# Attention followed by a gated feed-forward layer on one core: all transposes of rows and attention outputs move to TensorE

## The chip, the core and the metric

The kernel runs on one core of one Trainium2 chip. A core has five engines that run side by side, each with its own queue of instructions that it takes in order: TensorE (PE, matrix products and transposes, results in PSUM), VectorE (DVE), ScalarE (ACT), GpSimd (POOL), and SyncE (SP), which here only issues DMA transfers. The metric is the device time of one execution in microseconds (us), lower is better. The profile was taken from one execution by the hardware profiler.

## What is computed

The reference, cut to what matters (batch 8, 12 heads, 448 positions, head size 64; model size 768, inner size 2048):

```python
q_n, k_n = rmsnorm(q, g_q), rmsnorm(k, g_k)          # x / sqrt(mean(x*x) + 1e-6) * g
scores = q_n @ k_n.T / sqrt(64)
attn = softmax(scores)
x = (attn @ v)                                       # to (8*448, 768)
h = x @ w_in                                         # 768 -> 2048
out = (h * sigmoid(1.702 * h)) @ w_out               # 2048 -> 768, float32
```

Inputs are float32; the products are made in bfloat16 with float32 sums.

## The kernel before, in words

**Pairs.** The 8 x 12 heads are worked on as 48 pairs, `i` = 0 to 47, six pairs to a batch. The 128 partitions hold two heads of 64 where the head size lies on the partitions. A position is split as `ss * 4 + ns`, with 112 `ss` on the partitions and four `ns` along the row, so that 448 positions fill 112 partitions.

**One pair.** `load` (L869 for q and k, L867 for v) brings q, k and v, 224 KB each. `square` (L873 on POOL, L878 on ACT) and `reduce` (L887, DVE) give the sums of squares, and `seed`/`rsqrt` (or `by_log` for the first six pairs) one over the root. `norm` (L931, POOL or DVE) scales the rows and writes them as bfloat16 into a ring of three row buffers, `row_ring`. Rows have positions on the partitions; the score product needs the head size there. So each row buffer is **turned**: `T` in the plan, eight blocks of 112 x 128, four of Q and four of K.

- Pairs 0 to 11 (`ON_PE = NP * 2`): `turn_pe` (L954) does it by PE transposes into a PSUM bank, then two DVE copies bring it to SBUF: `take_q` (L958, called `KQ`) and `take_k` (L961, called `K`), the latter with the gains `gG` as a scale.
- Pairs 12 to 47: `turn_dma` (L966) issues one transposing DMA on SP, from the row buffer straight to SBUF. `scale_q` then multiplies Q by the gains in SBUF, on ACT (L973) or DVE (L975); this is `KQ` for these pairs.

`score` (`C`, L1001) multiplies Q and K on PE, `expo` (`E`, L1009 or L1011, ACT) takes the exponential, `values` (`P`, L1022, PE) multiplies by V with a column of ones that gives the sum, and `divide` (`O`, L1032 and L1033, DVE) writes the quotient into one of two buffers `obs`. The feed-forward layer needs this output turned once more (`B` and `X`): pairs 0 to 11 by `back_pe` (L1048, PE transposes into PSUM) and `take_x` (L1052, a DVE copy), pairs 12 to 47 by `back_dma` (L1055), one transposing DMA on SP.

**Feed-forward.** `first` (`F`, L1229) makes the 2048 inner columns of a batch in 16 groups, `tanh` (`H`, L1240, ACT) and `gate` (`G`, L1252, DVE) the gate. Tokens of two batches at a time go through `w_out`, plainly (`second`, L1260) or by a seven-product scheme on 2 x 2 blocks (`product`, L1325, with sums on DVE, L1316). The last two batches make `F` by such a scheme too (L1614). Results are copied out of PSUM by ACT or DVE and stored by SP (L1283).

**PSUM.** Two double banks hold scores, one bank `o` holds value products, and three banks `w` (two at the start) serve everything else: `F`, the output products, PE turns. A user holds its bank until its last reader is done: a PE turn of rows from the first transpose to the end of `K`, a turn back to the end of `X`. After the attention the score banks join the `w` banks.

**The order.** Nothing is scheduled on the fly. `ORDER` lists, engine by engine, every task's name in the order of its issue; `od.add` gives each task a cost, its dependencies and the PSUM or buffer slot that it takes, and `_Order.run` walks the lists with these costs. What comes out is the order in which the instructions are emitted, which free bank a task gets, and the filler matmuls (`fill`, L845) that go where the walk sees PE idle in the first 45 us. A name that stands in another engine's list than its `add` gives (`alt`) is made by that engine. The chip's times come from the chip: the lists fix only the order on each engine, and semaphores do the waiting.

Of the kernel before, what the change touches and what calls it, by code (L numbers as in the profile page):

```python
# [11 lines left out]
ALU = mybir.AluOpType  # L12
# [16 lines left out]
APART = 45000.0  # L29
APART = 45000.0  # L30
APART = 70000.0


class _Order:
# [36 lines left out]
    def run(self):  # L71
# [15 lines left out]
        lanes = []  # L87
# [37 lines left out]
        def begin(t):  # L125
# [4 lines left out]
            if t.eng == "POOL":  # L130
                when = max(when, hold)
            elif t.moves and len(lanes) >= LANES:
                when = max(when, lanes[-LANES].end)
# [12 lines left out]
        while emitted < len(self.tasks):  # L146
# [40 lines left out]
            if t.moves:  # L187
                t.rest, t.end = t.moves, NEVER
                t.there = free[eng] + (LANDS_SW if eng == "POOL" else LANDS)
                queues[{"POOL": "sw", "ACT": "act"}.get(eng, "hw")].append(t)  # L190
                if eng != "POOL":
                    lanes.append(t)
            else:
                finish(t, free[eng] + t.lat)
# [9 lines left out]
    def open(self, name, now):  # L204
# [5 lines left out]
        ('R', 0, 0), ('R', 0, 1), ('R', 1, 0), ('R', 1, 1), 'g', ('KQ', 0), 'gG', ('R', 3, 0),  # L210
        ('K', 0), ('R', 2, 0), ('N', 3, 0), ('N', 3, 1), ('KQ', 1), ('K', 1), ('V', 0), ('R', 4,
        0), ('KQ', 2), ('K', 2), ('V', 1), ('KQ', 3), ('K', 3), ('O', 0, 0, 0), ('R', 5, 0),
        ('X', 0, 0), ('O', 1, 0, 0), ('KQ', 4), ('K', 4), ('V', 3), ('O', 2, 0, 0), ('V', 4),
        ('X', 1, 0), ('KQ', 5), ('O', 3, 0, 0), ('X', 2, 0), ('V', 5), ('K', 5), ('O', 4, 0, 0),
        ('X', 3, 0), ('X', 4, 0), ('O', 0, 1, 0), ('R', 6, 0), ('R', 7, 0), ('X', 0, 1), ('O',
        5, 0, 0), ('X', 5, 0), ('R', 8, 0), ('Q0', 8), ('O', 1, 1, 0), ('G', 0, 0), ('X', 1, 1),
        ('G', 0, 2), ('O', 2, 1, 0), ('N', 6, 0), ('G', 0, 3), ('G', 0, 1), ('O', 3, 1, 0),
        ('X', 2, 1), ('KQ', 6), ('K', 6), ('G', 0, 4), ('O', 4, 1, 0), ('G', 0, 5), ('X', 3, 1),
        ('KQ', 7), ('K', 7), ('X', 4, 1), ('O', 5, 1, 0), ('V', 6), ('X', 5, 1), ('G', 0, 6),
        ('R', 9, 0), ('G', 0, 7), ('G', 0, 8), ('KQ', 8), ('K', 8), ('R', 10, 0), ('R', 11, 0),  # L220
        ('Q0', 11), ('G', 0, 10), ('O', 6, None, 0), ('G', 0, 9), ('V', 7), ('O', 7, None, 0),
        ('G', 0, 12), ('G', 0, 11), ('O', 7, None, 1), ('G', 0, 13), ('V', 8), ('G', 0, 14),
        ('KQ', 9), ('K', 9), ('R', 12, 0), ('G', 0, 15), ('O', 6, None, 1), ('KQ', 10), ('R',
        13, 0), ('K', 10), ('X', 6, None), ('R', 14, 0), ('O', 8, None, 0), ('Q0', 14), ('O', 9,
        None, 1), ('KQ', 11), ('K', 11), ('O', 8, None, 1), ('X', 7, None), ('R', 15, 0), ('X',
        8, None), ('R', 16, 0), ('O', 9, None, 0), ('V', 10), ('R', 17, 0), ('V', 11), ('Q0',
        17), ('O', 11, None, 0), ('X', 9, None), ('O', 11, None, 1), ('KQ', 13), ('O', 10, None,
        0), ('O', 10, None, 1), ('R', 18, 0), ('O', 12, None, 1), ('X', 10, None), ('R', 19, 0),
        ('X', 11, None), ('R', 20, 0), ('Q0', 20), ('N', 17, 0), ('O', 12, None, 0), ('G', 1,
        1), ('G', 1, 0), ('V', 14), ('N', 18, 1), ('G', 1, 2), ('G', 1, 3), ('O', 13, None, 1),  # L230
        ('TT', 0, 1), ('G', 1, 4), ('TT', 0, 0), ('TT', 1, 0), ('G', 1, 5), ('TT', 2, 0), ('G',
        1, 7), ('O', 13, None, 0), ('G', 1, 6), ('R', 21, 0), ('G', 1, 8), ('O', 14, None, 0),
        ('G', 1, 9), ('TT', 1, 1), ('TT', 3, 0), ('O', 14, None, 1), ('G', 1, 11), ('G', 1, 10),
        ('O', 15, None, 1), ('TT', 2, 1), ('G', 1, 12), ('TT', 3, 1), ('G', 1, 13), ('O', 15,
        None, 0), ('G', 1, 14), ('G', 1, 15), ('R', 22, 0), ('KQ', 18), ('S1', 0, 3), ('O', 16,
        None, 0), ('R', 23, 0), ('Q0', 23), ('S2', 0, 3), ('S3', 0, 3), ('U', 0, 3, 0), ('O',
        16, None, 1), ('X2', 0, 3), ('S4', 0, 3), ('O', 17, None, 1), ('N', 21, 0), ('X3', 0,
        3), ('S1', 0, 5), ('U', 0, 4, 1), ('O', 17, None, 0), ('X1', 0, 5), ('R', 25, 0), ('R',
        24, 0), ('U', 0, 3, 1), ('O', 18, None, 1), ('S2', 0, 5), ('R', 26, 0), ('KQ', 21),
        ('S3', 0, 5), ('Q0', 26), ('U', 0, 5, 0), ('O', 18, None, 0), ('S4', 0, 5), ('U', 0, 6,  # L240
        1), ('O', 19, None, 0), ('G', 2, 0), ('U', 0, 5, 1), ('R', 28, 0), ('O', 19, None, 1),
        ('R', 27, 0), ('G', 2, 2), ('V', 21), ('O', 20, None, 1), ('G', 2, 1), ('R', 29, 0),
        ('G', 2, 4), ('N', 26, 0), ('Q0', 29), ('G', 2, 3), ('O', 20, None, 0), ('G', 2, 5),
        ('G', 2, 6), ('G', 2, 7), ('O', 21, None, 0), ('R', 30, 0), ('G', 2, 8), ('V', 22),
        ('G', 2, 9), ('G', 2, 10), ('O', 21, None, 1), ('R', 31, 0), ('G', 2, 11), ('O', 22,
        None, 0), ('G', 2, 12), ('O', 22, None, 1), ('G', 2, 13), ('KQ', 26), ('N', 29, 0),
        ('G', 2, 14), ('G', 2, 15), ('O', 23, None, 1), ('R', 32, 0), ('S1', 1, 0), ('Q0', 32),
        ('S2', 1, 0), ('O', 23, None, 0), ('U', 1, 0, 0), ('S3', 1, 0), ('V', 25), ('O', 24,
        None, 1), ('R', 33, 0), ('O', 24, None, 0), ('X3', 1, 0), ('U', 1, 1, 1), ('O', 25,
        None, 0), ('U', 1, 2, 0), ('S4', 1, 0), ('KQ', 28), ('U', 1, 1, 0), ('N', 31, 1), ('V',  # L250
        26), ('O', 25, None, 1), ('G', 3, 0), ('R', 34, 0), ('U', 1, 0, 1), ('G', 3, 2), ('O',
        26, None, 1), ('R', 35, 0), ('G', 3, 1), ('G', 3, 3), ('G', 3, 4), ('O', 26, None, 0),
        ('Q0', 35), ('G', 3, 6), ('G', 3, 5), ('G', 3, 7), ('O', 27, None, 1), ('G', 3, 9),
        ('R', 37, 0), ('O', 27, None, 0), ('G', 3, 10), ('G', 3, 8), ('O', 28, None, 1), ('R',
        36, 0), ('G', 3, 12), ('G', 3, 11), ('O', 28, None, 0), ('R', 38, 0), ('Q0', 38), ('G',
        3, 13), ('O', 29, None, 0), ('G', 3, 14), ('G', 3, 15), ('S1', 1, 3), ('S2', 1, 3),
        ('U', 1, 3, 0), ('O', 29, None, 1), ('KQ', 32), ('S3', 1, 3), ('O', 30, None, 1), ('S4',
        1, 3), ('S5', 1, 2), ('X3', 1, 3), ('O', 30, None, 0), ('S1', 1, 5), ('U', 1, 4, 1),
        ('U', 1, 2, 1), ('KQ', 33), ('U', 1, 3, 1), ('S2', 1, 5), ('O', 31, None, 0), ('X1', 1,
# [402 lines left out]
def kernel(  # L662
# [22 lines left out]
    HALF = DM // 2  # L685
    WIN = 128
    AW = (NS - 1) * SS + WIN
    ON_PE = NP * 2
    EARLY = 4
    FILL, FILL_GAPS = 1.2, 0.6  # L690
    SINGLE = NP
# [1117 lines left out]
```

## Time and profile before

| what | value |
|---|---|
| median of 3 runs | 410.34 us (409.89 to 411.89) |
| the profiled execution | 410.82 us |
| its span, first to last instruction | 409.0 us |
| PE busy | 399.9 us, 98% |
| DVE, ACT, POOL busy | 308.1 (75%), 295.6 (72%), 197.7 us (48%) |
| PE transposes of rows, of outputs | 96 and 48 |
| transposing DMAs | 36 of rows, 36 of outputs |
| filler matmuls | 81, 11.8 us |
| granted PE clock | 0.999 |

A page of the profile gives the busy time of each engine, the span in 40 slices, the chain of work that ended last, and the costliest groups of instructions, each named by engine, line, operation and tiles. Other views give an engine's waits (who was waited for, total, number of times, longest), busy time by stretch of the span, and the timeline. PE's matmuls overlap each other: the duration of one is from its start to its modelled end, and the pace is read from start to start.

### The profile page before, as it was taken

What the parts mean: (1) busy time and instruction counts of PE and PEld (TensorE: products, weight loads), DVE (VectorE), ACT (ScalarE), POOL (GpSimd) and SP (SyncE); (2) the same over time, 40 slices, a digit from 0 to 9 for tenths busy, and PEclk for the clock granted to TensorE, in tenths of its full rate; (3) what the DMA queues carried; (4) which work ended last, traced back from release to release, by engine and by line L of the source; (5) the groups of instructions that cost most, each with busy time, mean ns of one, the idle gap of its engine ahead of it and who ended that gap; (6) DMA issues with size and microseconds to landing.
All of it is one profiled execution on the core that took longest, in us unless ns stands there. A gap on an engine that the chain in (4) does not pass through costs nothing.

```text
span 409.0 us, 9973 instructions
## 1 busy us (share of the span) xinstructions
PE 399.9 (98%) x3842; PEld 236.1 (58%) x3842; DVE 308.1 (75%) x624; ACT 295.6 (72%) x445; POOL 197.7 (48%) x289
## 2 busy tenths in 40 slices
PE   7899999999999999999999999999999999999996
PEld 6567886565555555555555555455455665555664
DVE  3997887778998597967686789887776788755353
ACT  4998899799898879766885668778888534685121
POOL 6787878874449657465884469343511200000000
PEclk9999999999999999999999999999999999999999
DMA  8999999999468977757766678656543113000244
GB/s 221 265 238 212 265 230 242 186 204 232 111 167 196 207 178 195 193 141 192 171 148 156 170 155 195 155 146 149 127 121 89 46 43 96 2 1 2 77 131 141
DMA packets 101776, 63.38 MB, mean 155 GB/s; under 512 B 55008, under 2 KB 101728, under 8 KB 101728
## 3 DMA queue, kind: packets, MB, share of 16 engines
q1 hardware_dynamic: 91840, 53.98, 54.7%
q0 software_dynamic: 7360, 6.29, 9.6%
q10 hardware_dynamic: 2528, 2.47, 2.3%
q8 instruction: 30, 0.49, 0.5%
q14 instruction: 18, 0.15, 0.2%
HBM read 45.61 MB, written 11.01 MB: 138 GB/s over the span
## 4 chain that ended last, share of the span: by engine, by line
PE 88%; DMA 6%; DVE 3%; ACT 1%; POOL 1%; SPq 0%; issue 0%; ACTq 0%; DVEq 0%; POOLq 0%
PE w L1229 25%; PE w L1325 22%; PE o L1022 12%; PE sc L1001 10%; PE b L1325 7%; PE b L1614 5%; PE w L1260 4%; DMA rows<-in_q_dram 3%; PE w L1614 3%; DMA rows<-in_k_dram 3%; DVE ssq L887 1%; PE w L954 1%; PE w L1048 1%; DVE g L1252 1%; ACT sq L878 0%; DVE obs L1033 0%
## 5 line engine op out<-in xcount | busy, mean ns | idle before, releaser
L1009 ACT ACTIVATE att<-sc 112x896 bf16<-112x896 f32 x168 | 145.8, 918 | 31.3 <-PE sc L1001 29.9
L1229 PE MATMUL w<-xt,w_in_s 128*128 128x448 bf16 (+1 forms) x672 | 121.5, 326 | 0.0
L1022 PEld LDWEIGHTS <-att 112*128 112x128 bf16 x1536 | 66.1, 98 | 34.2 <-issue 13.3
L1229 PEld LDWEIGHTS <-w_in_s 128*128 128x128 bf16 x672 | 60.2, 97 | 38.2 <-issue 5.0
L931 POOL TENSOR_TENSOR row<-rows,rs 112x512 bf16<-112x512 f32 x70 | 74.9, 1089 | 13.8 <-DMA qk<-row 9.7
L1252 DVE SCALAR_TENSOR_TENSOR g<-th,w 128x448 bf16<-128x448 f32 x96 | 58.0, 616 | 14.9 <-ACT th L1240 14.5
L1240 ACT ACTIVATE th<-w 128x448 f32<-128x448 f32 x96 | 50.9, 550 | 20.0 <-PE w L1229 16.5
L1022 PE MATMUL o<-vx,att 112*128 112x65 bf16 x1280 | 64.5, 194 | 0.6 <-DVE obs L1033 0.5
L887 DVE TENSOR_REDUCE ssq<-sq 112x16 f32<-112x1024 f32 (+1 forms) x50 | 57.9, 1168 | 6.6 <-ACT sq L878 5.7
L873 POOL TENSOR_TENSOR sq<-rows 112x512 f32<-112x512 f32 x37 | 39.7, 1090 | 21.4 <-DMA rows<-in_q_dram 12.5
L1001 PE MATMUL sc<-qk 64*128 64x448 bf16 (+1 forms) x360 | 47.4, 342 | 1.4 <-DVE qk L961 1.2
L944 POOL TENSOR_TENSOR vx<-rows,ones 112x512 bf16<-112x512 f32 x21 | 22.3, 1065 | 48.7 <-PE o L1022 40.8
L1033 DVE TENSOR_TENSOR obs<-o,rcp 112x256 bf16<-112x256 f32 x96 | 40.8, 425 | 3.3
L1325 PEld LDWEIGHTS <-late 128*128 128x128 bf16 x312 | 28.3, 97 | 19.7 <-issue 2.9
L1325 PEld LDWEIGHTS <-g 128*128 128x128 bf16 x288 | 26.0, 97 | 19.1 <-issue 4.0
L1032 DVE RECIPROCAL rcp<-o 112x4 f32<-112x4 f32 x96 | 17.2, 179 | 25.9 <-PE o L1022 25.2
L878 ACT ACTIVATE sq<-rows 112x1024 f32<-112x1024 f32 (+1 forms) x27 | 27.2, 1012 | 5.5 <-DMA rows<-in_q_dram 5.4
L1325 PE MATMUL w<-w_out_s,g 128*128 128x384 bf16 x152 | 29.4, 326 | 0.0
L920 POOL TENSOR_TENSOR t<-rs 112x48 f32<-112x48 f32 x28 | 9.2, 328 | 34.3 <-DVE rs L908 29.2
L1325 PE MATMUL w<-late 128*128 128x384 bf16 x136 | 25.7, 326 | 0.0
L1325 PE MATMUL w<-w_out_s,late 128*128 128x384 bf16 x128 | 24.1, 326 | 0.0
L1011 ACT ACTIVATE att<-sc 112x896 bf16<-112x896 f32 x24 | 20.6, 916 | 0.9 <-PE sc L1001 0.7
(133 smaller groups left out, 509.6 us busy)
## 6 DMA issues: line engine op xcount, KB each, us to landing
rows<-in_v_dram SPq DMA_DIRECT2D x42, 224.0 KB, 3.8
rows<-in_k_dram SPq DMA_DIRECT2D x41, 224.0 KB, 3.6
rows<-in_q_dram SPq DMA_DIRECT2D x41, 224.0 KB, 4.0
w_in_s<-in_moe_w_in_dram POOLq DMA_DIRECT2D x4, 768.0 KB, 10.7
w_out_s<-in_moe_w_out_dram POOLq DMA_DIRECT2D x4, 768.0 KB, 14.6
out_dram<-osb SPq DMA_DIRECT2D x14, 144.0 KB, 3.1
out_dram<-osb SPq DMA_DIRECT2D x10, 168.0 KB, 3.1
out_dram<-osb SPq DMA_DIRECT2D x11, 120.0 KB, 2.3
```

What stands on the lines that cost most here:

```text
L873: made = [nc.gpsimd.tensor_tensor(out=sq[i % N_SQ][:SS, g], in0=raw[turn(i, N_RAW, K_RAW)][:SS, g], in1=raw[turn(i, N_RAW, K_RAW)][:SS, g] ...
L887: nc.vector.reduce_sum(out=ssq_of[g0][:SS, i - g0, part], in_=sq[i % N_SQ][:SS, part], axis=AX.X)
L931: return eng.tensor_tensor(out=row_ring[i % N_QKN][:SS, gi].rearrange("p n (h d) -> p h n d", h=2), in0=raw[turn(i, N_RAW, K_RAW)][:SS, gi ...
L1001: nc.tensor.matmul(sc[:, hp, j * SH:j * SH + n], lhsT=qkw[r, k0:k0 + WIN], rhs=qk[r, 0, qs], start=True, stop=True)
L1009: nc.scalar.activation(out=att[:SS, t, :, :S], in_=sc, func=ACT.Exp)
L1022: nc.tensor.matmul(os_[u, w][:, x, :], lhsT=att_of(u)[:SS, kc, hp, qs * SS:qs * SS + WIN], rhs=vx_ring[turn(i, N_V, K_V)][:SS, hp, kc, :], ...
L1033: nc.vector.tensor_tensor(out=to[:SS, :, w, :] if h is None else to[:SS, :2].rearrange("p n h d -> p (n h) d"), in0=o[:SS, :, :D], in1=rcp ...
L1229: nc.tensor.matmul(gps[b, m][:, j * SH:j * SH + n], lhsT=w_in_s[:, ki, f * 128:(f + 1) * 128], rhs=xT[b][:, ki, lo:lo + n], start=(ki == 0 ...
L1240: nc.scalar.activation(out=th[:, :], in_=gps[b, m][:, :S], func=ACT.Tanh, scale=0.851)
L1252: nc.vector.scalar_tensor_tensor(out=g_of[b // 2][:, f:f + len(g), lo:lo + n], in0=view(ths.pop((b, m))[:, :]), scalar=1.0, in1=view(gps.p ...
L1325: nc.tensor.matmul(held[to], lhsT=lhs[:, ko, :], rhs=y[:, ko, :], start=first and ko == 0, stop=ko == NK - 1, skip_group_check=not first)
L1614: nc.tensor.matmul(joint[n, to][:, :S], lhsT=w[:, ki, n * 128:(n + 1) * 128], rhs=x[:, ki, :], start=first and ki == 0, stop=ki == KH - 1, ...
```

## The change

Pairs 12 to 47 are now turned like pairs 0 to 11. `turn_dma`, `back_dma`, `scale_q` and `ON_PE` are gone. Per touched pair PE makes eight transposes of rows and four of the output, and the three copies out of PSUM (`KQ`, `K`, `X`) are made by DVE or, for pairs from 6 on, by ACT where `ORDER` lists them there. An early half of a batch's first `F` now waits for all six `X` of the batch. All lists in `ORDER` are new. The walk's model of the DMA queues has another rule for when a transfer can be issued, and two assignments of `APART` that a third one overrides have another value.

How many tasks stand in each list, where the number differs:

| list | before | after |
|---|---|---|
| PE | `T` 24, `B` 18 | `T` 96, `B` 54 |
| DVE | `KQ` 25, `K` 12, `X` 18, `N` 19, `V` 23, `U` 41 | `KQ` 28, `K` 31, `X` 35, `N` 24, `V` 22, `U` 39 |
| ACT | `KQ` 23, `K` 0, `X` 0, `S` 29, `U` 16, `L` 8 | `KQ` 20, `K` 17, `X` 19, `S` 26, `U` 18, `L` 9 |
| SP | `T` 36, `X` 36, `L` 136 | `T` 0, `X` 0, `L` 135 |
| POOL | `N` 77, `S` 21, `V` 25 | `N` 72, `S` 24, `V` 26 |

(`U` are copies and sums of results; three copies `X1` to `X3` of partial products change sides as well.) The diff without the lists:

```diff
-    ON_PE = NP * 2
...
     def take_q(i):
+        if ("KQ", i) in ON:
+            nc.scalar.activation(out=qk_ring[turn(i, N_KZ, K_KZ)][:, 0], in_=tps[i][:, 0],
+                                 func=ACT.Identity)
+            return
         nc.vector.tensor_copy(out=qk_ring[turn(i, N_KZ, K_KZ)][:, 0], in_=tps[i][:, 0])
 
     def take_k(i):
+        if ("K", i) in ON:
+            nc.scalar.activation(out=qk_ring[turn(i, N_KZ, K_KZ)][:, 1], in_=tps[i][:, 1],
+                                 func=ACT.Identity, scale=gG[:, :])
+            return
         nc.vector.tensor_scalar(out=qk_ring[turn(i, N_KZ, K_KZ)][:, 1], in0=tps[i][:, 1],
                                 scalar1=gG[:, :], scalar2=None, op0=ALU.mult)
-    def turn_dma(i):
-        nc.sync.dma_start_transpose(
-            out=qkw_ring[turn(i, N_KZ, K_KZ)][:, :2 * S].rearrange("p (n s) -> p n s", s=SS),
-            in_=row_ring[i % N_QKN][:SS].rearrange("s g n c -> s (g n c)"))
...
     def take_x(u):
+        if ("X", *u) in ON:
+            nc.scalar.activation(out=columns(u), in_=tps.pop((u, "o")), func=ACT.Identity)
+            return
         nc.vector.tensor_copy(out=columns(u), in_=tps.pop((u, "o")))
-    def back_dma(u):
-        nc.sync.dma_start_transpose(
-            out=columns(u).rearrange("p (n s) -> p n s", s=SS),
-            in_=obs[place[u] % N_OBS][:SS].rearrange("s n h d -> s (n h d)"))
...
-        else:
-            od.add(("T", i, 1), "SP", 1350, lambda i=i: turn_dma(i), at - 10.0,
-                   deps=[("N", i, 0), ("N", i, 1)] + kz_free, moves=1600.0)
-            od.add(("KQ", i), "DVE", 335, lambda i=i: scale_q(i), at - 1.5, lock=True,
-                   alt=("ACT", 668, False),
-                   deps=[("T", i, 1), ("gG")])
...
+        od.add(("KQ", i), "DVE", 400, lambda i=i: take_q(i), at - 2.0,
+               alt=("ACT", 640, False) if i >= NP else None,
+               deps=[("T", i, 0)] + kz_free)
...
-        else:
-            od.add(("X", i, h), "SP", 1220, lambda u=u: back_dma(u), at - 10,
-                   deps=done_o + xt_free, moves=800.0)
...
     def project(b, m, kis):
...
-               deps=[("X", b * NP + p, None if b else m // 8) for p in kis]
+               deps=[("X", b * NP + p, None if b else m // 8) for p in (range(KI) if b else kis)]
```

## The prediction

> **What bounds the kernel now.** I read the page's busy shares first, then the slices, the chain that ended last, the waits of TensorE (PE), the busy time by stretch, and last a few microseconds of PE's timeline.
>
> ```profile
> PE 399.9 (98%) x3842; PEld 236.1 (58%) x3842; DVE 308.1 (75%) x624; ACT 295.6 (72%) x445; POOL 197.7 (48%) x289
> ...
> PE   7899999999999999999999999999999999999996
> ...
> PEclk9999999999999999999999999999999999999999
> ...
> PE 88%; DMA 6%; DVE 3%; ACT 1%; POOL 1%; SPq 0%; issue 0%; ACTq 0%; DVEq 0%; POOLq 0%
> ```
>
> PE is busy for 98% of the 409.0 us span, in every slice but the first and the last, at the full granted clock, and 88% of the chain that ended last is PE's own work. So idle time on PE is 409.0 - 399.9 = 9.1 us, and anything added to PE has nearly nowhere to hide. The waits of PE name what it lost time to (line, releaser: us in total, times, longest):
>
> ```profile
> PE w L954 <- POOL row L931: 1.4, 4, 0.8
> PE w L845 <- POOL ident masks.py:199: 1.4, 1, 1.4
> PE sc L1001 <- DVE qk L961: 1.2, 1, 1.2
> PE o L1022 <- DVE obs L1033: 0.8, 2, 0.5
> ```
>
> No transfer is in the list. The transposing DMAs run from 72.5 us (first of rows) to 331.8 us (last issue of an attention output), and PE never visibly waited for one. By stretch (us; PE, weight loads, DVE, ACT, POOL busy, then PE's clock, DMA share, GB/s):
>
> ```profile
> 35.00:100.00 65.00, 64.85 (x772) 44.71 (x771) 52.01 (x114) 56.58 (x80) 51.46 (x77) 1.00 1.09 224
> 100.00:200.00 100.00, 100.00 (x950) 54.79 (x948) 81.41 (x162) 81.39 (x118) 60.24 (x85) 1.00 0.73 177
> 200.00:300.00 100.00, 99.47 (x964) 54.64 (x962) 80.22 (x163) 75.61 (x110) 55.19 (x74) 1.00 0.65 155
> ```
>
> From 35 us to 300 us PE is idle for 0.15 + 0.00 + 0.53 = 0.7 us. That is the stage into which the change puts its work. (A busy matmul's modelled end reaches 0.2 to 0.3 us past its successor's start, so gaps shorter than that don't show; they bound nothing from below.)
>
> **Part 1: 432 transposes go to PE.** 36 pairs (12 to 47) are touched. Each needs 8 transposes for its rows (L954, four for Q and four for K) and 4 for its attention output (L1048). Their price is read from a stretch where the old kernel turns a pair on PE between matmuls of the value product:
>
> ```profile
> 68.98 0.29 PE L1022 MATMUL o<-late,att 112*128 112x65 bf16 x4
> 69.12 0.36 PE L954 MATMUL w<-ident,row 112*128 112x112 bf16 x4
> 69.31 0.29 PE L1022 MATMUL o<-late,att 112*128 112x65 bf16 x4
> 69.44 0.36 PE L954 MATMUL w<-ident,row 112*128 112x112 bf16 x4
> 69.64 0.42 PE L1022 MATMUL o<-late,att 112*128 112x65 bf16 x8
> ```
>
> The durations (0.36 us for four) overlap with what follows; the price is from start to start: 69.31 - 69.12 = 0.19 and 69.64 - 69.44 = 0.20, so 0.195 us for four, 49 ns each. A pair has three such groups: 3 x 0.195 = 0.585 us; 36 pairs: **21.1 us** (20.5 at 0.19, 21.6 at 0.20). Nothing on PE is taken away for it: what goes are DMA instructions of SP. Score matmuls cost extra when they begin after other work; they do so 105 times in the old PE list and 104 times in the new one, so the insertion adds nothing there.
>
> The row first: a transpose here lasts 213 ns from start to end and starts 49 ns after the one before, with the granted clock at 1.00 in the stretch from 35 to 100 us, which holds 82 of them. The Trainium skill ("TensorE: Matmul & The Clock Gate", section "Part 4: PE-mode transpose") speaks against the change: about 275 ns for one in a kernel's context, and a clock that transposes don't raise. By that figure 432 of them would be 119 us and the kernel near 530 us. The start-to-start row decides.
>
> **Part 2: the copies out of PSUM.** Before, each touched pair had one scaling of Q in SBUF (L973 on ACT, 23 times, L975 on DVE, 13 times). Now it has three copies from PSUM: Q (KQ), K with the scale, and X. From the two lists: DVE gains 16 Q copies, 19 K, 17 X and loses the 13 scalings; ACT gets 20 + 17 + 19 = 56 copies and loses 23 scalings.
>
> ```profile
> L973 ACT ACTIVATE qk<-qk,gG 128x448 bf16<-128x448 bf16 x23 | 15.4, 673 | 0.0
> L975 DVE TENSOR_SCALAR qk<-qk,gG 128x448 bf16<-128x448 bf16 x13 | 5.6, 433 | 0.0
> L958 DVE COPY qk<-w 128x448 bf16<-128x448 bf16 x6 | 2.3, 387 | 0.6 <-PE w L954 0.6
> L961 DVE TENSOR_SCALAR qk<-w,gG 128x448 bf16<-128x448 bf16 x6 | 2.7, 442 | 0.0
> L1052 DVE COPY xt<-w 128x448 bf16<-128x448 bf16 x6 | 2.3, 382 | 0.3 <-PE w L1048 0.3
> L1240 ACT ACTIVATE th<-w 128x448 f32<-128x448 f32 x96 | 50.9, 550 | 20.0 <-PE w L1229 16.5
> ```
>
> The last number before the second bar is the mean ns of one. DVE: 16 x 0.387 + 19 x 0.442 + 17 x 0.382 - 5.6 = +15.5 us. The re-drawn lists also move five normalisations (L931, 0.83 us each on DVE) from POOL to DVE, one value cast (0.68) and two output copies (0.55) off it: about +2 us more. ACT's copy of bf16 out of PSUM isn't in the trace; it lies between a 128x448 read of PSUM by ACT (L1240, 550 ns) and the SBUF scaling (L973, 673 ns), so 56 cost 31 to 38 us, less 15.4, less three squarings handed to POOL (3 x 1.06), plus a few output copies: +14 to +21 us. I take 0.6 us, +17. So DVE goes from 308 to about 326 us and ACT from 296 to about 313 us, each 72 to 75% of a 432 us span, as now. They grow as the span grows, and I count them at nothing; what they cover with is the idle quarter of both engines in the middle stages.
>
> **Part 3: waits that the change adds.** A turn of rows now holds one of the three PSUM banks `w`, from its first transpose to the end of the copy of K: at 69.12 to 70.65 us in the old trace, 1.5 us. A turn back holds one from 71.40 to 72.92 us, 1.5 us where the copy stood behind a 1.21 us reduction. 72 new holdings are about 108 bank-us over three banks for some 270 us, 13%. A transpose that finds no bank stops everything behind it on PE, since PE works in order. The bounds: nothing, and 72 x 0.49 = 35 us (the mean of the seven waits of PE listed above for another engine's data is (1.4 + 1.2 + 0.8) / 7 = 0.49 us). The nearest row is the stretch from 35 to 100 us, where the same code turns the rows of six pairs (48 transposes) and 34 transposes' worth of outputs, 82 transposes in 65 us (1.3 per us; after the change 432 in about 280 us, 1.5 per us): it lost 0.15 us. Scaled to 432 it is 0.8 us, which I take. The feed-forward task that starts early now waits for all six X of its batch instead of three; in the new list the nearest of them stand over 1 us of PE work ahead of it, so it costs nothing unless a copy is queued for longer.
>
> **Part 4: what goes.** 36 x 1.23 + 36 x 1.19 = 87 us of SP's issue time and 72 transfers that landed 3.2 us after their issue. Loads and stores pass SP's queue earlier; POOL's 9.7 us of waiting for the row buffers goes. Neither is late for PE now, so the gain is nothing; POOL is 48% busy, and what is late next for PE is still its own work.
>
> **Part 5: the start.** The order is re-drawn in all lists: the first w_in load goes to POOL's second place, loads swap queues, some copies of pairs 6 to 11 go to ACT. Up to 28 us PE spends 11.8 us on 81 filler matmuls (L845) beside real work, and most of the 9.1 us idle time is there too. ACT is the limit of that stage: 24 exponentials of 0.92 us in a row from 12.5 to 35 us, all kept. Bounds: 4 us gained or 2 us lost; I take zero.
>
> **Sum.** Against the profiled execution: 410.8 (span 409.0, 1.8 around it) + 21.1 + 0.8 = 432.7 us. Its time stands 0.5 above the median of 410.3, so the forecast is **432.2 us**.
>
> **Rivals.**
> - *Waits take over.* The banks, or copies late on a more loaded DVE or ACT, stop PE. For: three banks serve everything, the banks of feed-forward results are emptied through both engines, and DVE and ACT stand at 81% in 100 to 200 us. Against: 35 to 100 us with turns and 0.15 us idle. One in three of the 72 holdings at 0.49 us is 12 us: 444 us.
> - *The start gives part back.* If the new order fills a quarter to a half of the filler and idle time with real work (5 to 10 us of 20.9), it ends at 422 to 427 us. Against: the exponentials that limit that stage all stay.
> - *Not slower.* The one mechanism: real work takes the place of the filler at the start. All of it is 11.8 + 9.1 = 20.9 us against 21.1 us added, so it decides only when the start yields more than 19 us; with everything recovered the kernel ends at 411 us, no change. A gain isn't reachable by this, since the idle time isn't there.
> - That it doesn't do what it says can't be: both DMA functions are deleted.
>
> **Chances.** Forecast, 429 to 436 us: 0.66. Waits, 436 to 470: 0.21. Part of the start back, 413 to 429: 0.10. Not slower: 0.03, of which 0.01 faster. 0.5% of 410 us is 2 us, about what a measurement of this kernel can tell from no change. The range 428 to 440 us takes in the forecast's case, the lower part of the waits and the top of the start's: about 0.8.
>
> **What would show it.** In the profile after: 576 transposes instead of 144 (384 of rows, 192 of outputs), still 49 ns apart; no transposing DMA; PE busy around 421 us at 97 to 98%; DVE about 326, ACT about 313; idle PE between 35 and 320 us below 3 us; the last stage, from the last output copy on, as long as before (about 77 us). Part 3 is wrong if PE's waits list ACT or DVE copies for more than 3 us; part 5 if filler matmuls fall well below 81; part 1 if transposes start more than 55 ns apart.

## The result and the profile after

The changed kernel takes **445.87 us** (median of 4 runs, 443.89 to 448.13), the kernel before beside it on the same chip 411.12 us (409.89 to 411.96): a ratio of 1.085 with a 95% interval of 1.0785 to 1.0914, 34.75 us slower. The forecast was 432.2 us with a range of 428 to 440: slower, as said, but 13.7 us more than said, and above the range. The profiled execution took 445.17 us, with a span of 443.4 us.

The page after: busy times, PE's slices, its clock, and the shares of the chain that ended last.

```profile
PE 426.8 (96%) x4286; PEld 262.3 (59%) x4286; DVE 325.2 (73%) x664; ACT 310.6 (70%) x478; POOL 199.5 (45%) x291
...
PE   7689999999999999999999999999999989999996
...
PEclk9889999999999999999999999999999999999999
...
PE 89%; DMA 3%; ACT 3%; DVE 2%; issue 1%; POOL 1%; SPq 0%; ACTq 0%; DVEq 0%; POOLq 0%
```

DVE and ACT stand where the forecast put them (326 and 313). PE is busier than the forecast's 421 us, although it has only the 432 transposes and 12 filler matmuls more (4286 - 3842 = 444), and its second slice is a 6 where it was an 8 before. The clock dips in the second and third slice (11 to 33 us). The waits of PE (line, releaser: us in total, times, longest):

```profile
PE w L968 <- DVE row L945: 2.9, 2, 2.7
PE w L968 <- POOL row L945: 2.6, 2, 2.4
PE b L1055 <- ACT att L1016: 1.8, 1, 1.8
PE w L1073 <- DVE g_row L1065: 1.4, 1, 1.4
PE w L859 <- POOL ident masks.py:199: 1.4, 1, 1.4
PE w L1255 <- ACT late L980: 0.7, 1, 0.7
PE w L968 <- ACT qk L973: 0.6, 2, 0.3
PE w L968 <- DVE qk L976: 0.6, 3, 0.2
PE w L968 <- ACT late L973: 0.2, 1, 0.2
```

The first three are longer than any wait before. The two at the top are transposes that wait for normalised rows (`row`), and the timeline puts both in the first 24 us, among pairs that were turned on PE before too. The third is a transpose of an output that waits for an exponential, at 357 us. Waits for copies that empty a bank (the last four lines) come to 2.1 us. By stretch (us; PE, weight loads, DVE, ACT, POOL busy, clock, DMA share, GB/s), the start first and then the middle:

```profile
10.00:15.00 5.00, 4.08 (x46) 2.99 (x46) 3.35 (x8) 1.95 (x5) 2.04 (x2) 1.00 1.17 263
15.00:20.00 5.00, 2.34 (x18) 1.80 (x17) 3.49 (x6) 1.11 (x3) 1.93 (x2) 0.74 1.16 276
20.00:25.00 5.00, 2.65 (x23) 1.63 (x22) 1.70 (x2) 4.00 (x7) 2.04 (x2) 0.84 1.16 273
25.00:30.00 5.00, 4.98 (x68) 3.13 (x67) 4.42 (x12) 4.80 (x9) 4.38 (x5) 0.74 1.17 259
...
35.00:100.00 65.00, 64.14 (x830) 47.47 (x828) 52.20 (x113) 56.76 (x80) 49.08 (x73) 1.00 0.84 183
100.00:200.00 100.00, 99.92 (x1010) 58.22 (x1009) 82.83 (x161) 81.48 (x125) 53.51 (x77) 1.00 0.39 114
200.00:300.00 100.00, 99.03 (x1029) 58.27 (x1028) 77.55 (x162) 74.33 (x110) 62.16 (x81) 1.00 0.37 109
```

Two of these stretches in the kernel before:

```profile
15.00:20.00 5.00, 4.52 (x69) 3.02 (x70) 4.70 (x11) 4.97 (x9) 4.98 (x6) 1.00 1.13 262
20.00:25.00 5.00, 4.95 (x89) 3.20 (x85) 4.89 (x15) 4.81 (x8) 4.90 (x6) 1.00 1.18 238
```

From 15 to 25 us PE, DVE and POOL all lose much of their time after the change, and ACT too until 20 us, while the DMA is as full as before (share above 1, near 270 GB/s). ACT's two longest waits in 11 to 21 us, 2.98 and 4.83 us, are put down to loads of k: the engines wait for data. From 25 to 30 us PE is busy again, but at a mean granted clock of 0.74: the clock row is at 0.50 from 17.4 to 20.8 us and from 24.2 to 27.6 us. From 100 to 300 us PE shows hardly any idle time.

How late this stage is can be read from the 24 exponentials of the first pairs (ACT; duration in ns, then first and last start in us), before and after:

```profile
L1011 ACT ACTIVATE att<-sc x24: 897/918/940, 12.5 to 40.8; 112x896 bf16<-112x896 f32 x24
L1018 ACT ACTIVATE att<-sc x24: 897/917/951, 21.0 to 49.1; 112x896 bf16<-112x896 f32 x24
```

The first starts 8.5 us later than before and the last 8.3 us later. From there to the end of the span it is 368.2 us before and 394.3 after, 26.1 more.

**An account of PE's time.** A busy matmul's modelled end covers gaps up to about 0.16 us (a transpose lasts 213 ns and the next one starts after 49), so I also added up PE's time from the start of one instruction to the start of the next. Each such time is put down to the instruction up to its own pace in the trace (49 ns for 112 columns, 191 ns for 448; about 95 ns more where scores begin after other work or end), and what is over is lost time; stretches behind a filler matmul are counted apart, with the idle time in them.

| us | before | after | difference |
|---|---|---|---|
| matmuls that both kernels have | 372.1 | 370.6 | -1.5 |
| transposes | 7.6 | 29.7 | +22.1 |
| filler stretches, all before 40 us | 14.4 | 22.4 | +8.1 |
| lost between other instructions | 9.5 | 14.7 | +5.2 |
| start of the last matmul | 404.96 | 438.80 | +33.8 |

(A stretch of 1.4 us ahead of the first matmul completes each column. The first two rows belong together: some gaps move from one group to the other, and the sum, 20.6 us, is what the work grew by. Some 1.2 us of the lost time after the change stand in 24.2 to 27.6 us, where the clock was halved.) So there are three things to explain: some 21 us of transposes, 8 us at the start, 5 us of waits.

Two theories. **A, lists:** the start is late because the new lists bring weights and loads in another order; the transposes themselves cost what Part 1 says. **B, transposes:** the turns cost more than their pace (their weight loads, banks, the clock), and the copies behind them stop PE. B would let each transpose cost (33.8 / 432) 78 ns.

### The profile page after: what moved, and what is told of

Its sections match the earlier page's. It is cut to its first block, busy times and chain, and to the rows that moved or that the text cites. A ratio compares the mean times of both kernels' runs of the same rounds, so it can differ in the third digit from the quotient of the medians.

```text
span 443.4 us, 10799 instructions
## 1 busy us (share of the span) xinstructions
PE 426.8 (96%) x4286; PEld 262.3 (59%) x4286; DVE 325.2 (73%) x664; ACT 310.6 (70%) x478; POOL 199.5 (45%) x291
## 2 busy tenths in 40 slices
DMA packets 51091, 51.04 MB, mean 115 GB/s; under 512 B 4320, under 2 KB 51040, under 8 KB 51040
## 4 chain that ended last, share of the span: by engine, by line
PE 89%; DMA 3%; ACT 3%; DVE 2%; issue 1%; POOL 1%; SPq 0%; ACTq 0%; DVEq 0%; POOLq 0%
PE w L1224 24%; PE w L1320 20%; PE o L1029 12%; PE sc L1008 10%; PE b L1320 5%; PE w L968 4%; PE b L1609 4%; PE w L1255 4%; DMA rows<-in_k_dram 3%; PE w L1609 3%; PE w L1055 2%; ACT att L1016 1%; DVE row L945 1%; DVE g L1247 0%; POOL row L945 0%
## 5 line engine op out<-in xcount | busy, mean ns | idle before, releaser
L1016 ACT ACTIVATE att<-sc 112x896 bf16<-112x896 f32 x168 | 147.0, 917 | 31.5 <-PE sc L1008 30.8
L945 POOL TENSOR_TENSOR row<-rows,rs 112x512 bf16<-112x512 f32 x67 | 71.1, 1076 | 41.2 <-PE w L968 29.3
L1029 PEld LDWEIGHTS <-att 112*128 112x128 bf16 x1536 | 68.2, 98 | 27.0 <-issue 10.4
L1247 DVE SCALAR_TENSOR_TENSOR g<-th,w 128x448 bf16<-128x448 f32 x96 | 57.7, 615 | 15.7 <-ACT th L1235 14.7
L1029 PE MATMUL o<-vx,att 112*128 112x65 bf16 x1280 | 68.8, 195 | 0.1
L887 POOL TENSOR_TENSOR sq<-rows 112x512 f32<-112x512 f32 x45 | 48.9, 1106 | 7.4 <-ACT qk L980 3.7
L968 PE MATMUL w<-ident,row 112*128 112x112 bf16 x384 | 32.7, 216 | 6.8 <-DVE row L945 2.9
L1320 PEld LDWEIGHTS <-late 128*128 128x128 bf16 x304 | 27.6, 97 | 16.9 <-issue 0.7
L968 PEld LDWEIGHTS <-row 112*128 112x128 bf16 x384 | 23.2, 99 | 15.9 <-issue 5.2
L892 ACT ACTIVATE sq<-rows 112x1024 f32<-112x1024 f32 (+1 forms) x23 | 23.0, 1002 | 11.4 <-DMA rows<-in_q_dram 7.6
L1320 PE MATMUL w<-late 128*128 128x384 bf16 x144 | 27.7, 325 | 0.0
L934 POOL TENSOR_TENSOR t<-rs 112x48 f32<-112x48 f32 x28 | 7.8, 278 | 41.1 <-DVE rs L922 37.8
```

Source lines behind the costliest of these rows:

```text
L887: made = [nc.gpsimd.tensor_tensor(out=sq[i % N_SQ][:SS, g], in0=raw[turn(i, N_RAW, K_RAW)][:SS, g], in1=raw[turn(i, N_RAW, K_RAW)][:SS, g] ...
L945: return eng.tensor_tensor(out=row_ring[i % N_QKN][:SS, gi].rearrange("p n (h d) -> p h n d", h=2), in0=raw[turn(i, N_RAW, K_RAW)][:SS, gi ...
L968: nc.tensor.transpose(tps[i][:, gi, s, :], row_ring[i % N_QKN][:SS, gi, s, :], ident[:SS, :SS])
L1016: nc.scalar.activation(out=att[:SS, t, :, :S], in_=sc, func=ACT.Exp)
L1029: nc.tensor.matmul(os_[u, w][:, x, :], lhsT=att_of(u)[:SS, kc, hp, qs * SS:qs * SS + WIN], rhs=vx_ring[turn(i, N_V, K_V)][:SS, hp, kc, :], ...
L1247: nc.vector.scalar_tensor_tensor(out=g_of[b // 2][:, f:f + len(g), lo:lo + n], in0=view(ths.pop((b, m))[:, :]), scalar=1.0, in1=view(gps.p ...
```

## Experiments

Each was timed against the kernel before on the same chip; the changed kernel is taken at 445.87. The experiments ran on several chips, with medians of the kernel before from 410.1 to 411.3 us, so two experiments are compared to within about 1 us.

**1. The transposes alone, in the old kernel.** Six transposes of a constant ahead of the scores of each even `t`, into the score bank that the scores overwrite: 432 in all, no copies, no bank held longer, old lists.

```diff
+        if i >= 2 * NP and t % 2 == 0:
+            idle = sc[:, 0, :].bitcast(BF16)
+            for s in range(6):
+                nc.tensor.transpose(idle[:, s * SS:(s + 1) * SS], ident[:SS, :], ident[:SS, :SS])
```

> The kernel before with 432 extra transposes on PE and nothing else: at the start of each score task of pairs 12 to 47, six transposes of the identity go into the score bank that the task has taken, and the scores overwrite them. No copies, no new bank, no new wait, the same order. Theory (each transpose on a full PE costs its 49 ns): 432 x 49 = 21 us, 431 to 433 us. Rival (the rest of the 35 us also comes from PE's extra work, by a slower pace or a clock that falls): 440 to 446 us.

Measured: 431.91 us against 411.03, ratio 1.051 (1.0481 to 1.0539): **+20.9 us**, 48 ns a transpose. In its profile PE's work grew by the same 20.7 us (399.9 before):

```profile
PE 420.6 (98%) x4274; PEld 259.8 (60%) x4274; DVE 309.9 (72%) x624; ACT 297.6 (69%) x445; POOL 197.2 (46%) x289
```

B's first half falls: the transposes cost their pace, with the clock at 1.00 from 100 to 300 us. The Trainium skill ("TensorE: Matmul & The Clock Gate", section "Part 4: PE-mode transpose"), weighed in the prediction, gives about 275 ns for one, by which 432 would have been an estimated 119 us. A transpose lasted 212 ns here, but the next one didn't wait for its end; the measurement decides.

**2. Only the outputs back to DMA.** Experiment 4's kernel (below) with the outputs of pairs 12 to 47 turned by `back_dma` again; the rows stay on PE. The lists from 40 to 365 us are re-drawn for it.

```diff
-        od.add(("B", i, h), "PE", 210 if h is None else 110, lambda u=u: back_pe(u), at + 1.5,
...
+        if i in OUTS_DMA:
+            od.add(("X", i, h), "SP", 1220, lambda u=u: back_dma(u), at - 10,
+                   deps=done_o + xt_free, moves=800.0)
```

> Half of the change: rows of all pairs are turned on PE, the outputs of pairs 12 to 47 by DMA again as in the kernel before; weights as in e1, and the lists between 40 and 365 us re-drawn for it. Against e1 (440.3 us): theory (PE pays 49 ns for each transpose, and a turn back needs a bank): 144 x 49 = 7.1 us less, and the 2 us wait for a bank goes, 430 to 433.5 us. Rival (each removed turn gives back more, in proportion to the 29 us that e1 stands above the kernel before, a third of them): 430 or less; rival (DMA turns bring waits of their own and the gain is lost): 436 or more.

Measured: 433.28 us (432.51 to 433.46), ratio 1.0534 (1.0503 to 1.0564), 7.06 us less than experiment 4's 440.34; by the two ratios, since the chips differ, it is 7.9 us. 144 transposes at 49 ns are 7.1 us, so the price holds for the change's own transposes too. The comparison doesn't price copies and banks apart, since the lists are re-drawn: by the account the transposes take 7.2 us less and the stretch from 350 to 366 us loses 1.4 us less, while 40 to 80 us loses 1.4 us more.

**3. The weights early, in the old kernel.** In the changed kernel's trace POOL issues the first two quarters of `w_in` at 5.5 us; before, the first one went at 16.5 us (start, us, instruction; the line of after, then that of before):

```profile
5.53 1.77 POOL L1192 DMA_DIRECT2D w_in_s<-in_moe_w_in_dram  x2
```

```profile
16.50 0.92 POOL L1197 DMA_DIRECT2D w_in_s<-in_moe_w_in_dram  x1
```

A quarter is 768 KB, and the first pairs' q, k and v (224 KB each) are under way at that time. By the packets of the trace, from 10 to 20 us after the change the weights' queue moves 219 to 242 KB in every 2.5 us and the loads' two queues 362 to 442, where these moved 625 to 663 alone before. POOL's own time for the two issues (1.77 us) isn't the cause: behind them it stood idle for 4.4 us, until 11.7 us. So the old kernel was given early weights and nothing else. They come somewhat earlier there than in the changed kernel (issues at 4.0, 4.9, 13.6 and 24.0 us, against 5.5, 6.5, 18.1 and 27.6), so the price comes out rather high:

```diff
-        ('S', 1, 1), ('N', 0, 0), ('N', 0, 1), ('N', 1, 1), ('N', 1, 0), ('N', 2, 0), ('N', 2,
-        1), ('WI', 0), ('V', 2), ('N', 4, 1), ('N', 4, 0), ('WI', 1), ('N', 5, 0), ('N', 5, 1),
-        ('S', 6, 0), ('S', 7, 0), ('WI', 2), ('S', 8, 0), ('WI', 3), ('Q', 8), ('N', 6, 1),
+        ('WI', 0), ('WI', 1), ('S', 1, 1), ('N', 0, 0), ('N', 0, 1), ('N', 1, 1), ('N', 1, 0),
+        ('WI', 2), ('N', 2, 0), ('N', 2, 1), ('V', 2), ('N', 4, 1), ('N', 4, 0), ('WI', 3),
+        ('N', 5, 0), ('N', 5, 1), ('S', 6, 0), ('S', 7, 0), ('S', 8, 0), ('Q', 8), ('N', 6, 1),
```

> The kernel before with one edit, the reverse: the first two w_in loads stand first in POOL's list, the other two a little earlier. Theory (early weights starve the first loads): the first exponentials stall, 415 to 420 us. Rival (the order of the other lists is the cause): 411 us, no change.

Measured: 418.72 us against 411.03, ratio 1.0189 (1.016 to 1.0218): **+7.7 us** with no turn added. The clock falls in its start as well, and once more later:

```profile
10.00:15.00 5.00, 4.58 (x36) 2.83 (x36) 3.01 (x5) 3.52 (x7) 3.92 (x4) 0.68 1.16 270
40.00:45.00 5.00, 5.00 (x61) 4.36 (x61) 3.66 (x10) 2.72 (x5) 2.57 (x10) 0.75 0.00 0
```

Not all of the 7.7 us is filler. By the account the filler stretches grow by 3.7 us, to 18.1, and lost time by 4.6: PE stops once for 2.4 us ahead of 38.7 us, and the half clock from 39.1 to 42.5 us costs some 1.5. The last of the 24 exponentials starts at 49.1 us, 8.3 later than before.

**4. The weights later, in the changed kernel.** The other way round: `WI` and `WO` go back to about their old places in POOL's list.

```diff
-        ('S', 0, 1), ('WI', 0), ('WI', 1), ('N', 1, 0), ('N', 1, 1), ('N', 3, 1), ('WI', 2),
-        ('N', 2, 0), ('N', 2, 1), ('N', 4, 0), ('N', 4, 1), ('WI', 3), ('V', 4), ('V', 3), ('N',
...
+        ('S', 0, 1), ('N', 1, 0), ('N', 1, 1), ('N', 3, 1), ('N', 2, 0), ('N', 2, 1), ('WI', 0),
+        ('N', 4, 0), ('N', 4, 1), ('WI', 1), ('V', 4), ('V', 3), ('N', 5, 0), ('V', 5), ('S', 6,
```

> The changed kernel with one edit: the first four w_in and the first two w_out loads stand later in POOL's list, where the kernel before has them. Theory (the start lost about 8 us because two w_in transfers were issued at 5.5 us and from 9.5 us on shared the DMA engines with the first loads of q, k and v): the second pair's scores start near 16 us instead of 23.8, and the kernel takes 436 to 439 us. Rival (the new order of the other lists, not the weights, makes the late start): the scores stay near 23 us and the time near 445.

Measured: 440.34 us (439.51 to 442.28), ratio 1.0725 (1.0687 to 1.0763): 5.5 us less than the changed kernel, short of the 436 to 439 expected. Its profile shows the same: the scores of the second pair start at 18.7 us, after 23.8 in the changed kernel and 13.6 before, and the last of the 24 exponentials at 44.6 us, after 49.1 and 40.8. By the account its filler stretches are 18.3 us, between 22.4 and 14.4. The weights are the larger part of the late start, not all of it. The half clock is gone from its start too (a mean of 0.999, after 0.992).

**5. The new order of the first loads, in the old kernel.** What else differs at the start is the order of the first loads on ACT and SP (SP takes `L 4 0` in place of `L 2 2`, ACT `L 1 2` and `L 5 2`, and more of that kind); weights as before, no turns.

```diff
-        ('L', 0, 0), ('L', 1, 0), ('L', 3, 1), ('L', 2, 1), ('S', 0, 0), ('S', 0, 1), ('S', 1,
-        0), ('Q', 0), ('L', 4, 1), ('L', 4, 0), ('L', 5, 0), ('S', 3, 0), ('Q', 1), ('S', 2, 0),
+        ('L', 1, 0), ('L', 0, 0), ('L', 3, 1), ('S', 0, 0), ('L', 2, 1), ('L', 5, 0), ('S', 0,
+        1), ('L', 4, 1), ('S', 1, 0), ('Q', 0), ('S', 3, 0), ('Q', 1), ('L', 1, 2), ('L', 5, 2),
...
-        ('L', 0, 1), ('L', 1, 1), ('L', 3, 0), ('L', 2, 0), ('L', 2, 2), ('L', 1, 2), ('L', 0,
-        2), ('L', 7, 0), ('L', 5, 1), ('L', 8, 0), ('L', 3, 2), ('L', 5, 2), ('L', 6, 1), ('L',
+        ('L', 0, 1), ('L', 1, 1), ('L', 3, 0), ('L', 2, 0), ('L', 4, 0), ('L', 5, 1), ('L', 0,
+        2), ('L', 2, 2), ('L', 3, 2), ('L', 7, 1), ('L', 6, 0), ('L', 6, 1), ('L', 7, 0), ('L',
```

> The kernel before with the new order of the first loads of q, k and v on SP and ACT (pair 1 before pair 0, k of pair 2 behind the first square), weights where they were. Theory (the order of the loads is the part of the late start that moving the weights did not give back, 3 to 4 us): 413.5 to 416 us. Rival (it is the order of the computing tasks): 410 to 412 us.

Measured: 414.56 us (413.21 to 416.73) against 411.34, ratio 1.0079 (1.0047 to 1.0112): **+3.2 us**; filler stretches 18.6 us by the account, as in experiment 4. The last of the 24 exponentials starts at 44.0 us, 3.2 later than before, as much as the kernel lost. Weights and loads are each enough for a late start without any turn. No run gave the old kernel both, and their prices don't add up (7.7 + 3.2 is more than 8); that both delay the same first pairs is the likely reason.

**6. One issue off ACT.** In the trace after, ACT issues pair 4's v load (`L 4 2`) and computes nothing for 4.8 us. I wondered whether that instruction held ACT up. It was moved to SP.

```diff
-        ('S', 2, 0), ('Q', 3), ('L', 4, 2), ('E', 0, 0, 1), ('Q', 2), ('S', 4, 0), ('E', 0, 0,
+        ('S', 2, 0), ('Q', 3), ('E', 0, 0, 1), ('Q', 2), ('S', 4, 0), ('E', 0, 0,
...
-        2), ('L', 2, 2), ('L', 3, 2), ('L', 7, 1), ('L', 6, 0), ('L', 6, 1), ('L', 7, 0), ('L',
+        2), ('L', 2, 2), ('L', 3, 2), ('L', 4, 2), ('L', 7, 1), ('L', 6, 0), ('L', 6, 1), ('L',
```

> The changed kernel with one edit: the load of v of pair 4, at whose issue ACT stood from 16.1 to 20.6 us ahead of its first exponential, goes to SP behind the load of v of pair 3. Theory (slow transfers): the exponential starts up to 4 us earlier, but the next loads are as late, and at least half of the 8 us stays: 440 to 445 us. Rival (that one issue in ACT's queue is the late start): 437 to 439 us.

Measured: 444.57 us (442.15 to 445.57), ratio 1.0812 (1.0771 to 1.0854), 1.3 us less, with ranges that overlap. The first exponential started 4.0 us earlier (17.0), the last of the 24 only 1.3 us (47.8). The issue isn't the cause; the loads are late.

**7. Two loads moved on top of experiment 4.** Pair 2's k load one place earlier on ACT, pair 4's v load to SP as in experiment 6.

```diff
-        ('L', 1, 0), ('L', 0, 0), ('L', 3, 1), ('S', 1, 0), ('L', 2, 1), ('L', 5, 0), ('S', 0,
+        ('L', 1, 0), ('L', 0, 0), ('L', 3, 1), ('L', 2, 1), ('S', 1, 0), ('L', 5, 0), ('S', 0,
```

> The kernel with the weights later (e1), and two loads moved: the load of k of pair 2 is issued third on ACT's queue, ahead of the first square, as in the kernel before (4.8 us there, 8.3 us in e1), and the load of v of pair 4 leaves ACT for SP, where it does not stand ahead of the first exponential. Theory (what e1 leaves of the late start, 3.9 us less PE work done by 35 us than before, is these two issues): the second pair's scores start near 16 us instead of 18.7, 437 to 438.5 us, 2 to 3 us less than e1. Rival (it is the rest of the order): 440 us, as e1.

Measured: 440.79 us (439.88 to 441.89), ratio 1.0728 (1.0672 to 1.0785): no change from 440.34. The guess at which loads matter was wrong: pair 2's k was asked for earlier, but the first exponential started at 16.5 us instead of 15.9.

**8. The whole start of before.** The changed kernel with the old order of every engine for the first 32 us. The head of PE's list:

```diff
-        'gT', ('T', 0, 0), ('T', 0, 1), ('T', 1, 0), ('C', 0, 0, 1), ('C', 0, 0, 0), ('T', 1,
+        ('T', 0, 0), 'gT', ('T', 0, 1), ('C', 0, 0, 0), ('T', 1, 0), ('T', 1, 1), ('C', 0, 0,
```

> The changed kernel with the whole start of the kernel before: on every engine the tasks that the old order begins in its first 32 us come first, in the old order, and the new lists follow without them. Theory (beside 21 to 22 us of PE turns, all of the start's 8 us comes from the new order of loads and weights, the rest from waits in the middle): the start is as before, and the kernel takes 435 to 438 us, some 4 us less than with the weights alone moved. Rival (the start is slow for another reason, as the copies of pairs 6 to 11 or the turns themselves): 440 us or more.

Measured: 441.80 us (439.99 to 443.46), ratio 1.0749 (1.0688 to 1.081): 4.1 us less, not the 8 to 11 expected. Filler stretches are down to 16.5 us, but lost time is up from 14.7 to 16.6: where the old start meets the new order, new waits stand (PE's, of this kernel):

```profile
PE w L860 <- DVE g L1248: 2.0, 1, 2.0
PE b L1056 <- ACT att L1017: 1.8, 1, 1.8
PE w L1225 <- DMA w_in_s<-in_moe_w_in_dram: 1.4, 1, 1.4
```

The first and the third are new: the weights of the first batch are late at 29 us, its gate at 35 us. The last of the 24 exponentials starts at 46.4 us, later than in experiment 4 (44.6), though the first starts at 12.8.

**9. The seam re-drawn.** Experiment 8 with the order from 24 to 75 us drawn anew.

```diff
-        ('R', 3, 0), ('KQ', 0), ('K', 0), ('R', 2, 0), ('N', 3, 0), ('KQ', 1), ('K', 1), ('KQ',
+        ('K', 0), ('R', 2, 0), ('N', 3, 0), ('N', 3, 1), ('KQ', 1), ('K', 1), ('V', 0), ('R', 4,
...
-        ('X', 0, 1), ('X', 5, 0), ('R', 8, 0), ('Q0', 8), ('O', 1, 1, 0), ('G', 0, 1), ('G', 0,
+        5, 0), ('R', 8, 0), ('X', 5, 0), ('O', 1, 1, 0), ('G', 0, 0), ('Q0', 8), ('X', 1, 1),
```

> The changed kernel with the old start (e5, 441.8 us), and the order between 24 and 75 us re-drawn so that the old start and the new lists meet without the two waits that PE had there (1.6 us for the weights, 2.2 us for a gate). Theory (the start was late because of its own lists, and what is left are the turns and 4 to 5 us of waits): 436.5 to 439 us. Rival (the stage behind the start is late for another reason): 441 or more.

Measured: 440.91 us (438.26 to 442.56), ratio 1.0712 (1.0664 to 1.0759): again short by the median. By the account its filler stretches are 15.7 us, 6.7 less than in the changed kernel, but lost time is 18.9, 4.2 more. Some 1.7 of these 4.2 aren't the order's: in this profiled execution, the longest of the four (442.56), the clock was halved from 356.8 to 360.2 us, where eight matmuls of 384 columns took 2.55 us instead of 1.30.

```profile
355.00:360.00 5.00, 4.69 (x38) 2.83 (x38) 3.40 (x6) 1.35 (x3) 0.00 (x0) 0.68 0.02 3
```

The execution whose mean granted clock was 1.000 took 438.26 us, inside the expected range. So the theory isn't refuted by this experiment; what is shown is that part of what the start gives is lost again behind it, some 2.8 us by the account between 30 and 80 us.

**10. Two outputs by DMA at the end of the attention.** At 357 us PE stops for 1.8 us at an output turn (timeline of the changed kernel: start, duration, instruction, wait):

```profile
356.59 0.55 PE L1008 MATMUL sc<-qk 64*128 64x448 bf16 x4
358.96 0.36 PE L1055 MATMUL b<-ident,obs 112*128 112x112 bf16 x4 [1.82 <-ACT att L1016]
```

The turn's tile is named `b`, a former score bank: all three `w` banks are held by output products that aren't finished, and PE waits until the exponential has read a score bank. In experiment 8's kernel the outputs of pairs 44 and 45 went back to DMA, which takes no bank.

> The kernel with the old start, and the attention outputs of pairs 44 and 45 turned by DMA again, everything else on PE. Those are the two turns back that come while all three PSUM banks are held by unfinished output products; in the changed kernel PE stood for 1.8 us ahead of the first, until the score banks came free. Theory (a bank is missing there): 1.8 us plus eight transposes of 49 ns, 2 to 3 us less than the kernel with the old start. Rival (that wait hides other work's lateness): 0.4 us less, the transposes alone.

Measured: 439.55 us (438.27 to 440.78), ratio 1.0689 (1.0644 to 1.0734), 2.25 us less than experiment 8, with ranges that overlap a little, and the wait is gone from the list. About 0.4 us of it are the eight transposes saved; the rest fits the wait of 1.8 us, and the account has 1.5 us less lost from 350 to 366 us.

**11. Half of every copy of rows, in the changed kernel.** For pairs 12 to 47 only half the columns of Q and K are copied out of PSUM; the other half of what the scores read is old data. This part of the computation is left out.

```diff
+        n = slice(0, NS // 2 if i >= 2 * NP else NS)
...
-            nc.scalar.activation(out=qk_ring[turn(i, N_KZ, K_KZ)][:, 1], in_=tps[i][:, 1],
+            nc.scalar.activation(out=qk_ring[turn(i, N_KZ, K_KZ)][:, 1, n], in_=tps[i][:, 1, n],
```

> The changed kernel with shorter copies: of the turned rows of pairs 12 to 47 only half of the columns of Q and of K are copied out of PSUM, so the other half of what the scores read is left out (old data); all transposes, waits and the order stay. It takes some 0.2 to 0.3 us from each of 72 copies on DVE and ACT, and lets each bank go earlier. Theory (the re-drawn order hides the copies; besides the start and the turns only some 3 us of waits and 2 us for a missing bank are lost after 60 us): 443 to 446 us, at most 3 us less than the changed kernel's 445.9. Rival (the copies' time is the rest, as the kernel before with more copies suggests): 441 us or less.

Measured: 443.69 us (442.08 to 446.23), ratio 1.0803 (1.0744 to 1.0863): 2.2 us less, with ranges that overlap. Half the columns don't halve the time (on DVE 271 ns against 385, on ACT 360 against 545, plain copies), and the copies of outputs stay whole. So shorter copies are worth some 2 us, not clear of the noise, and what copies cost in all isn't bounded by this run.

**12. More copies in the old kernel.** A second pass in place behind each of the 23 scalings of Q on ACT, and behind each of the 72 quotients of pairs 12 to 47 on DVE. The values stay the same.

```diff
             nc.scalar.activation(out=t, in_=t, func=ACT.Identity, scale=gG[:, :])
+            nc.scalar.activation(out=t, in_=t, func=ACT.Identity)
...
+        if i >= 2 * NP:
+            nc.vector.tensor_scalar(out=to[:SS, :, w, :], in0=to[:SS, :, w, :], scalar1=1.0,
+                                    scalar2=None, op0=ALU.mult)
```

> The kernel before with copy work added on ACT and DVE, and nothing on PE: each of ACT's 23 scalings of Q is followed by a copy in place (0.67 us each, 15 us), and each of the 72 quotients of pairs 12 to 47 on DVE by a multiplication by one in place (about 0.2 to 0.25 us each, 14 to 18 us). Theory (the idle quarter of both engines covers the copies): 411 to 413 us. Rival (the copies, not the transposes, cost the rest of the 35 us): 415 us or more.

Measured: 422.39 us against 410.83, ratio 1.0274 (1.0233 to 1.0315): **+11.6 us**, and the expectation falls. PE has no more work than before; yet it waits for DVE, over the whole middle (the last line is the added pass on DVE, with its busy time in us and the mean ns of one):

```profile
PE o L1023 <- DVE obs L1034: 2.3, 5, 1.1
PE w L1233 <- DVE g L1256: 1.4, 4, 0.5
L1038 DVE TENSOR_SCALAR obs<-obs 112x256 bf16<-112x256 bf16 x72 | 29.3, 407 | 2.5
```

A pass took 407 ns, not the 0.2 to 0.25 us expected, so DVE's load was about twice the expected one: it stands at 332 us, 24 more than before, where the change added 17; ACT at 307 has 11 more, where the change added 15. These passes lengthen the way from a product to its output, and the old order has no room for that. So idle shares of 25% and 28% don't hide copies by themselves. Whether their place or their larger sum did it, this run doesn't tell apart.

## Why the prediction was right in its side and wrong in its size

- **Part 1 (21.1 us) was right.** 576 transposes, 49 ns from start to start; +20.9 us for 432 alone in the old kernel, 7.1 to 7.9 us for 144 of the change's own, and 20.6 us in the account.
- **Part 2 (copies at nothing) was nearly right for this kernel, for a reason that it gave too simply.** The engines' totals came out at 325 and 311 us against 326 and 313, and PE's waits for copies at 2.1 us. "The idle quarter of both engines" isn't enough, as +11.6 us in experiment 12 shows, with a larger load on DVE in an order not drawn for it. That the new lists hide the copies because they were drawn for them is argued, not shown.
- **Part 3 (0.8 us for waits) was too small.** Lost time grew by 5.2 us. Of it some 2 us stand between 350 and 366 us, almost all at the missing bank (experiment 10), 1.1 between 60 and 80 us, and the rest is spread in pieces of a fraction of a microsecond, many at the first transpose of a turn. Its test didn't see this: copies in PE's waits came to 2.1 us (less than 3), and visible idle time from 35 to 300 us to 0.86 + 0.08 + 0.97 = 1.9 us. The row it was scaled from (35 to 100 us, 0.15 us idle) showed visible idle time only, too (the modelled ends hide 0.16 us for nearly every matmul, not the 0.2 to 0.3 it read); and it couldn't show the end of the attention, where output products fill the banks.
- **Part 4 (nothing gained by the removed DMAs) stands**: no transfer was in PE's waits before, and DMA packets fell from 101776 to 51091 without a stage that grew shorter.
- **Part 5 failed: "Bounds: 4 us gained or 2 us lost; I take zero."** The start lost 8 us. The prediction saw that "the first w_in load goes to POOL's second place" and looked only at ACT's exponentials, "all kept". They were kept, but they need q and k first, and they ran from 21.0 to 49.1 us instead of 12.5 to 40.8. The weights share the DMA with q and k (the share was above 1 already in this stage), so two early transfers of 768 KB hold the first loads back: +7.7 us in the old kernel with weights even earlier, 5.5 us less in the changed kernel with weights later. The order of the first loads alone is worth 3.2 in the old kernel. The half clock has a part in this (some 1.2 us of lost time in 24.2 to 27.6 us); what it cost in all isn't priced apart. The sign of the test was wrong too: it watched for fewer filler matmuls than 81, and there were 93. Two readings of the start were off as well: only 19 of the 24 exponentials start by 35 us in the kernel before, and only 4.3 of the 9.1 us of idle time stand before 28 us (3.8 are in the last 77).

With the 8 and the 4.4 us that Part 3 fell short (5.2 - 0.8), 432.2 becomes 444.6, against 445.87 measured. The rival "waits take over" named 444 us, which is near by luck: its mechanism wasn't the larger one, since waits for banks and copies are 5 us at most.

**What stays open.** No version was found in which the old start and the new middle go together: experiments 8 and 9 bring most of the filler stretches back and lose 2 to 4 us elsewhere, part of it at a half clock in experiment 9. The clock is a rival for some of these microseconds that no experiment holds fixed: experiment 8's kernel took 439.99 and 441.10 us in the two executions with a mean granted clock of 1.000, and 442.51 and 443.46 with 0.992, and the changed kernel had 0.988 to 0.992 in all four. How much of the 8 us a better start could return for good isn't settled, nor is the cause of each of the small losses in the middle. The kernel before remains the fastest of all that ran.

## What to carry to other kernels

Where one engine is busy to 98%, work moved to it costs its full pace from start to start, however cheap it is beside a DMA; read that pace from a stretch of the same trace, and here it predicted to within a microsecond in twenty. When a change re-draws an order, price the first loads apart: list what is issued to the DMA in the first microseconds before and after, and look at who shares it with the data that the first products need. Idle shares of other engines say that there is room, not where: a copy in the way of the bound engine needs its room at its own point in the order.

## What the runs showed of the hardware

- The granted clock fell in starts that waited for data: 0.74, 0.84 and 0.74 after the change (15 to 30 us), 0.68 in experiment 3 (10 to 15 us), with 1.00 in the same stretches of the kernel before. It also fell where PE was busy again after a stop, to 0.75 in experiment 3 (40 to 45 us, after a stop of 2.4 us) and 0.68 in experiment 9 (355 to 360 us, after one of 1.8 us); a stop of 1.8 us at 357 us after the change had no such fall. It stood at 1.00 in 100 to 300 us, with transposes strewn among products.
- A weights transfer from POOL's queue took 219 to 242 of 604 to 676 KB moved in 2.5 us, a third or a little more, beside loads from two other queues, ACT's and SP's. In the kernel before, from 20 to 27.5 us, with SP's queue alone beside it, it took 296 to 308 of 564 to 601 KB, a half. The Trainium skill ("DMA: Bandwidth & Descriptors", section "SWDGE vs HWDGE vs iDMA") says that a DMA engine goes round its queues in turn; one of three queues would get a third by that, and the trace agrees. So a late, large transfer isn't behind the early ones, it is among them.
- ACT's copy of 128 x 448 bf16 out of PSUM took 545 ns plain and 635 ns with a scale per partition, below its 673 ns for scaling the same tile in SBUF.
